# fp32 for y in the early tiles, splits only where they are needed, and another order of the third expert's units

## The chip, the cores and the metric

One core of one Trainium2 chip. The metric is the device time of one execution in microseconds; the profile is that of one execution of the same program. PE is the matrix engine, PEld its weight loads, DVE VectorE, ACT ScalarE, POOL GpSimd, SP the sync engine.

## The reference, cut to what matters

```python
# attention: B, H, S, D = 4, 8, 768, 48; a state of D x D per head, complex decay
scale = np.minimum(mag, 0.999) / (mag + 1e-06)
for t in range(S):
    S_re, S_im = ar * S_re - ai * S_im + k[t] (x) v[t], ar * S_im + ai * S_re
    y[t] = q[t] @ S_re
# first mixture, x (3072, 384), 8 experts of 1024, all of them on all rows
P = sinkhorn(exp(x @ w_gate - max), 8 rounds)          # columns and rows by turns
out = sum_e P[:, e] * (relu(x @ w1[e]) @ w2[e])
# second mixture: each row by the one expert of its largest logit
```

All is fp32. The kernel may split a value into two f16 parts, high and residue, and multiply three products of the parts.

## The kernel before, in words

The 3072 rows are 24 tiles of 128; tile n is step c = n // 4 of 128 time steps of batch b = n % 4. The kernel has a first and a second part. In the first, under `first_phase`, attention runs tile by tile and three of the eight experts of the first mixture (`RAW`) are computed without their factors, since the factors come only from the Sinkhorn loop at its end. The second part adds up these three with their factors, computes the other five, routes, and computes the second mixture.

In the first part the order of PE is that of the code (`manual_schedule`); DVE, ACT and the DMA queues are ordered by a planner, which follows priorities (`high_priority` shifts them) and the order of emission.

- `prep(u)` does a pair of tiles (u = 0 and 1 alone): decay, the scans over 128 steps, and WW, from which `stack` builds Q and K of a tile by DMA (SP's queue) in one of two buffers. It is a generator; its labels ("d", "s", "c1", ...) say how far it is. The planes, WW and v16 have one buffer each.
- `scales(u, ss)` turns the sums of squares of q, k and v into powers of two, and carries a bound of the state.
- `tile_attn(n)` has five steps: scores of heads 0 to 3 (ps, L393), masked and split into sc (L396 to L399); the same of heads 4 to 7; residues of S and Q (L402, L403), and K transposed (pk, kt); y (L420) out of three f16 products of Q and S (from tile 4 on) and three of sc and v; U (L427, fp32) and the new state.
- `emit_x` scales y's rows, splits them, transposes them into xg and computes the gate's logits.
- `tile_unit(e, n, wt, L)` is one expert on L tiles: for L = 2 four z steps (18 matmuls of 256 columns each) and two y steps (24 of 384), so six steps. `work` is the queue of units, `step(k)` emits the next k steps. `add_work(n)` puts two units (experts 0 and 1) in the queue for a pair of tiles, and, once the third expert's weights are there (`third_ready`, after 25 pieces of `early2`, one per attention step from tile 4 on), up to two of the third expert's from the list `third`.
- Tiles 0 to 3 follow the written list of letters: S stack, t attention step, x a step of emit_x, A add_work, w a unit step, p, a, b a step of a prep, e a piece of the weights. From tile 4 on a loop does it: after each attention step unit steps, in tile n's loop the rest of emit_x of tile n - 1, and prep of the pair after.
- At the end: one unit step, the last units, one unit of the last pair ahead of the others, two units to their end; then `sinkhorn`, nine times a piece of it, a piece of expert 3's weights and one unit step; then the units that are left.

Of the kernel before, what the change touches and what calls it, by code (L numbers as in the profile page):

```python
# [8 lines left out]
F32 = mybir.dt.float32  # L9
# [4 lines left out]
ALU = mybir.AluOpType  # L14
# [5 lines left out]
P = 128  # L20
# [2 lines left out]
PR = 128  # L23
HEAD_OF_SLOT = [0, 2, 4, 1, 3, 5, 6, 7]
RAW = 3
NS1 = 12
NS = 28
NSX = 31
# [4 lines left out]
class Kernel:  # L33
# [215 lines left out]
    def prep_part(self, u, L, a, qk, T, r, A, X, v, v16, WW):  # L249
# [2 lines left out]
        R = 3 * L  # L252
        tt = nc.vector.tensor_tensor
        stt = nc.vector.scalar_tensor_tensor
        ss = self.sm.tile([P, 3], F32, name=f"ss{u}", tag="ss")
        yield from self.decay(u, a, X, r)
        for i, src in enumerate((qk[:, 0], qk[:, 1], v)):
            dst = X[:, 0].rearrange("p (n w) -> p n w", w=384) if i == 2 else X[:, 0]
# [1 line left out]
        yield "d"  # L260

        def scaled():
            sc = self.scales(u, ss)
            self.act(u, v16[:, 0], v, AF.Copy, scale=sc[:, 1:2])
            stt(out=v16[:, 1], in0=v, scalar=sc[:, 1:2], in1=v16[:, 0], op0=ALU.mult, op1=ALU.subtract)
            self.vs.update((u + k, (v[:, k], v16[:, :, k], sc)) for k in range(L))

        if u > 1:
# [71 lines left out]
    def scales(self, u, ss):  # L340


        nc = self.nc
        ts = nc.vector.tensor_scalar
        ps = self.pp.tile([P, 3], F32, name=f"qkv{u}", tag="ps")
        nc.tensor.matmul(ps, self.ones, ss, start=True, stop=True)
        h, sc = (self.sm.tile([P, 5], F32, name=f"{t}{u}", tag=t) for t in ("sch", "scs"))
        bound = self.bound[u // 2 % 2]
        ts(out=h[:, 0:3], in0=ps, scalar1=2.0 ** -60, scalar2=None, op0=ALU.max)
        ts(out=h[:, 0:3].bitcast(I32), in0=h[:, 0:3].bitcast(I32), scalar1=1, scalar2=0x7F800000,  # L350
           op0=ALU.logical_shift_right, op1=ALU.bitwise_and)
        ts(out=h[:, 0:3], in0=h[:, 0:3], scalar1=2.0 ** 64, scalar2=None, op0=ALU.mult)
        nc.vector.scalar_tensor_tensor(out=bound, in0=h[:, 1:2], scalar=h[:, 2:3], in1=bound, op0=ALU.mult, op1=ALU.add)
        ts(out=h[:, 3:4].bitcast(I32), in0=bound.bitcast(I32), scalar1=0x7F800000, scalar2=None, op0=ALU.bitwise_and)
        nc.vector.tensor_copy(h[:, 1:2], h[:, 2:3])
        ts(out=h[:, 2:3], in0=h[:, 3:4], scalar1=2.0, scalar2=None, op0=ALU.mult)
        nc.vector.reciprocal(out=sc[:, 0:3], in_=h[:, 0:3])
        ts(out=sc[:, 0:3], in0=sc[:, 0:3], scalar1=2.0 ** 14, scalar2=None, op0=ALU.mult)
        ts(out=sc[:, 3:4], in0=sc[:, 2:3], scalar1=h[:, 1:2], scalar2=2.0 ** -14, op0=ALU.mult, op1=ALU.mult)
        ts(out=sc[:, 3:4], in0=sc[:, 3:4], scalar1=sc[:, 0:1], scalar2=None, op0=ALU.mult)  # L360
        ts(out=sc[:, 4:5], in0=h[:, 3:4], scalar1=h[:, 0:1], scalar2=2.0 ** -27, op0=ALU.mult, op1=ALU.mult)
        return sc

# [9 lines left out]
    def tile_attn(self, n):  # L373

        nc = self.nc
        c, b = divmod(n, 4)
        ap, ap2 = self.ap, self.ap2
        Q, K = self.QK[n % 2][:, 0], self.QK[n % 2][:, 1]
        tt = nc.vector.tensor_tensor
        stt = nc.vector.scalar_tensor_tensor  # L380
        v, v16, scl = self.vs.pop(n)
        last = c == NC - 1
        if c > 0:
            Q16 = self.q16[:, 0:2048].rearrange("p (a h t) -> p a h t", a=2, h=8)
            S16 = self.q16[:, 2048:2816].rearrange("p (a w) -> p a w", a=2)
            nc.scalar.activation(S16[:, 0], self.S[b], AF.Copy, scale=scl[:, 2:3])
            nc.scalar.activation(Q16[:, 0], Q[:, :, 0:128], AF.Copy, scale=scl[:, 0:1])
        sc = ap.tile([P, 2, 2, 4, P], F16, name=f"sc{n}", tag="sc")
        for g in range(2):
            ps = self.pp.tile([P, 4, P], F32, name=f"ps{n}_{g}", tag="ps")  # L390
            for j in range(4):
                h = g * 4 + j
                nc.tensor.matmul(ps[:, j, :], K[:, h, 0:128], Q[:, h, 0:128], start=True, stop=True)  # L393
            with self.tc.high_priority(offset=200):
                sc32 = self.UV.rearrange("p c w -> p (c w)")[:, 0:512].rearrange("p (h t) -> p h t", h=4)
                stt(out=sc32, in0=ps, scalar=scl[:, 3:4], in1=self.mask[:, None, :].to_broadcast([P, 4, P]), op0=ALU.mult,  # L396
                    op1=ALU.mult)
                nc.scalar.copy(sc[:, g, 0], sc32)
                tt(out=sc[:, g, 1], in0=sc32, in1=sc[:, g, 0], op=ALU.subtract)  # L399
            yield  # L400
        if c > 0:
            stt(out=S16[:, 1], in0=self.S[b], scalar=scl[:, 2:3], in1=S16[:, 0], op0=ALU.mult, op1=ALU.subtract)  # L402
            stt(out=Q16[:, 1], in0=Q[:, :, 0:128], scalar=scl[:, 0:1], in1=Q16[:, 0], op0=ALU.mult, op1=ALU.subtract)  # L403
        if not last:
            kt = ap.tile([P, 8, PR], F32, name=f"kt{n}", tag="kt")
            for g in range(2):
                pk = self.pp.tile([P, 4, PR], F32, name=f"pk{n}_{g}", tag="ps")
                for j in range(4):
                    nc.tensor.transpose(pk[:, j, :], K[:, g * 4 + j, 0:128], self.id32[:PR, :PR])
                nc.scalar.copy(kt[:, g * 4:g * 4 + 4, :], pk)  # L410
        yield
        y = self.pp.tile([P, 384], F32, name=f"y{n}", tag="ps")
        cols = [slice(HEAD_OF_SLOT[s] * 48, HEAD_OF_SLOT[s] * 48 + 48) for s in range(8)]
        own = [slice(s * 48, s * 48 + 48) for s in range(8)]
        for s in range(8):
            z = [(0, 0), (0, 1), (1, 0)]
            mm = [(Q16[:, i, s, :], S16[:, j, own[s]]) for i, j in z] if c > 0 else []
            mm += [(sc[:, s // 4, i, s % 4, :], v16[:, j, cols[s]]) for i, j in z]
            for i, (l, r) in enumerate(mm):
                nc.tensor.matmul(y[:, cols[s]], l, r, start=(i == 0), stop=(i == len(mm) - 1))  # L420
        self.pend = self.emit_x(n, y, scl[:, 4:5])
        next(self.pend)
        yield
        if not last:
            U = self.pp.tile([PR, 384], F32, name=f"U{n}", tag="ps")
            for s in range(8):
                nc.tensor.matmul(U[:, own[s]], kt[:, s, :], v[:, cols[s]], start=True, stop=True)  # L427
            UV = self.UV
            if c == 0:
                nc.scalar.copy(UV[:, 0], U)  # L430
            else:
                tt(out=UV[:, 0], in0=U, in1=self.S[b], op=ALU.add)
            nc.scalar.copy(UV[0:48, 1], UV[64:112, 0])
            nc.scalar.copy(UV[64:112, 1], UV[0:48, 0])
            e4 = UV.rearrange("p c (h e) -> p c h e", e=48)
            tt(out=e4, in0=e4, in1=self.QK[n % 2][:, :, :, 128:129].to_broadcast([PR, 2, 8, 48]), op=ALU.mult)
            tt(out=self.S[b], in0=UV[:, 0], in1=UV[:, 1], op=ALU.add)
        yield
# [660 lines left out]
    def first_phase(self):  # L1099
# [5 lines left out]
        with ExitStack() as ctx:  # L1105
# [3 lines left out]
            with ExitStack() as actx:  # L1109
# [24 lines left out]
                def add_work(n):  # L1134
# [7 lines left out]
                    if n % 2 == 1:  # L1142
                        third.append(n - 1)
                        if third_ready:
                            for _ in range(2):
                                if third:
                                    k = third.pop(0)
                                    work.append(self.tile_unit(2, k, self.wts[2], 2))

                self.WW = WW = {}  # L1150
                self.vs = {}
                first = [self.prep(u) for u in range(2)]
                prep = None
                for e in range(RAW):
# [7 lines left out]
                attn, pend, self.pend = {}, {}, None  # L1162
                at = None
                for what in """w a a a b a w e e a a e g w e w a e a e S0 e e b b b t0 b b r2 b w e t0 w t0 e w e e t0 x0
                      p t0 p A0 b S1 p x0 b t1 e w t1 e w t1 t1 w e w w e r4 S2 t1 e w e x1 t2 p A1 e w t2
                      w p x1 e t2 t2 w w p x2 t2 S3 e w p w x2 e t3 t3 e w A2 w t3 t3 A3 w w t3 x3 e w e x3""".split():
                    n = int(what[1:] or 0)
                    if what == "e":
                        next(early, None)
# [23 lines left out]
                run(early)  # L1193
                for n in range(4):
                    run(pend[n])
                while at in (None, "d1", "d2", "d"):
                    at = next(prep)
                for n in range(4, NT):
# [22 lines left out]
                    for i, _ in enumerate(self.tile_attn(n)):  # L1221
                        if early2 is not None and n > 3 and next(early2, True):
                            early2 = None
                            third_ready.append(True)
                        step(2 if i != 2 or len(work) > 4 else 1)
                        if ahead and i in (0, 2):
                            next(ahead, None)
                            if i == 0:
# [3 lines left out]
                    step(1)  # L1232
                was = len(work)
                add_work(NT - 1)
                work.insert(1, work.pop(was))
                run(work.pop(0))
                run(work.pop(0))
                late = self.getw(RAW, first_w)
                for _ in self.sinkhorn():
# [192 lines left out]
```

## Time and profile before

| | |
|---|---|
| time, median of 3 runs | 2129.28 us (2127.75 to 2132.78) |
| the profiled execution | 2127.34 us, span 2125.6 us |
| mean granted TensorE clock | 0.969 |
| busy: PE, PEld | 1935.3 us (91%), 1291.1 us (61%) |
| busy: DVE, ACT, POOL | 1285.5 us (60%), 887.7 us (42%), 202.4 us (10%) |
| busy tenths of PE in the first 8 of 40 slices | 1 4 6 8 9 6 8 9 |
| of DVE in the same | 8 8 9 9 9 9 9 8 |

The span runs from the first to the last instruction; the time of an execution has a little around it. A matmul's record is longer than the time until the next one starts, so lengths of PE work are read from start to start. The first part ends at about 889 us.

### The profile page before, as it was taken

To read this page: it belongs to the slowest core of one execution; us is meant where nothing else is said; L and a number is where in the kernel's file an instruction comes from. 1 tells how busy PE (TensorE), PEld (TensorE's weight loads), DVE (VectorE), ACT (ScalarE), POOL (GpSimd) and SP (SyncE) were. 2 spreads that over 40 slices of the span, in tenths; PEclk is the share of its full clock that TensorE was granted. 3 is DMA by queue.
4 is the path that set the end of the run, shared out by engine and by line. 5 is a ranking of instruction groups with operands and counts; after the bars stand their busy time and mean duration, and the time that the engine had idled before them with its cause. 6 is when DMAs were issued, how large, how long until landed. Compare 5 with 4: busy or idle time off the path is not lost.

```text
span 2125.6 us, 38747 instructions
## 1 busy us (share of the span) xinstructions
PE 1935.3 (91%) x15202; PEld 1291.1 (61%) x15202; DVE 1285.5 (60%) x3008; ACT 887.7 (42%) x1678; POOL 202.4 (10%) x311
## 2 busy tenths in 40 slices
PE   1468968999999996989999999999999999989998
PEld 1357757777778774635555555555555555567885
DVE  8899999988895326155434443443444355565886
ACT  5665655555454323243433433333334223355111
POOL 1000000000000000101100110110011010100005
PEclk9689889999999998989999999999999999999999
DMA  4323342422223102174311330231133200144222
GB/s 164 116 77 115 102 124 70 133 70 73 65 72 111 62 24 75 57 246 142 120 60 60 119 119 30 90 119 60 60 119 112 97 31 16 43 141 144 102 84 91
DMA packets 72927, 197.33 MB, mean 93 GB/s; under 512 B 10467, under 2 KB 54511, under 8 KB 67872
## 3 DMA queue, kind: packets, MB, share of 16 engines
q0 software_dynamic: 21808, 104.85, 14.2%
q1 hardware_dynamic: 50928, 89.88, 13.8%
q8 instruction: 127, 2.08, 0.4%
q14 instruction: 64, 0.52, 0.1%
HBM read 122.74 MB, written 53.71 MB: 83 GB/s over the span
## 4 chain that ended last, share of the span: by engine, by line
PE 53%; DMA 3%; DVE 2%; issue 1%; ACT 1%; SPq 1%; POOL 0%; DVEq 0%; POOLq 0%; ACTq 0%
PE ym L531 21%; PE z L520 20%; PE y L871 5%; PE z L856 4%; DMA rr<-rawd 1%; DMA late<-srt 1%; PE yt L566 1%; SPq L588 1%; PE zt L555 1%; DVE wt L134 0%; PE pt L651 0%; DMA st<-in_w_dram 0%; DVE acc L599 0%; ACT x L839 0%; DVE h L577 0%
## 5 line engine op out<-in xcount | busy, mean ns | idle before, releaser
L531 PE MATMUL ym<-wt,h 128*128 128x384 f16 x2880 | 477.5, 326 | 0.0
L531 PEld LDWEIGHTS <-h 128*128 128x128 f16 x2880 | 280.4, 98 | 184.8
L520 PEld LDWEIGHTS <-wt 128*128 128x128 f16 x2160 | 211.4, 99 | 262.9 <-issue 22.6
L577 DVE SCALAR_TENSOR_TENSOR h<-z,h 128x512 f16<-128x512 f32 (+1 forms) x352 | 212.2, 604 | 244.6 <-ACT h L576 237.2
L576 ACT ACTIVATE h<-z 128x512 f16<-128x512 f32 (+1 forms) x352 | 184.7, 526 | 373.3 <-PE z L520 242.2
L555 PE MATMUL zt<-xg,wt 128*128 128x256 f16 (+1 forms) x2736 | 303.2, 270 | 0.0
L566 PE MATMUL yt<-wt,ht 128*128 128x384 f16 x1728 | 290.4, 326 | 3.7 <-DVE ht L577 3.3
L555 PEld LDWEIGHTS <-wt 128*128 128x128 f16 x2736 | 259.4, 100 | 30.3
L520 PE MATMUL z<-xl,wt 128*128 128x512 f16 x1080 | 244.8, 386 | 14.1 <-DVE h L577 10.9
L520 PE MATMUL z<-xg,wt 128*128 128x512 f16 x1080 | 238.6, 379 | 0.0
L566 PEld LDWEIGHTS <-ht 128*128 128x128 f16 x1728 | 167.8, 98 | 111.9 <-DVE ht L577 5.9
L604 DVE SCALAR_TENSOR_TENSOR acc<-ym,pf,acc 128x384 f32<-128x384 f32 x120 | 74.0, 617 | 264.4 <-PE ym L531 264.4
L577 DVE SCALAR_TENSOR_TENSOR ht<-zt,ht 128x512 f16<-128x512 f32 x144 | 98.8, 686 | 73.6 <-ACT ht L576 72.9
L856 PE MATMUL z<-x,late 128*128 128x128 f16 x2016 | 130.6, 219 | 9.7 <-DVE late L845 7.0
L393 PE MATMUL ps<-QK 128*128 128x128 f32 x384 | 61.8, 310 | 84.4 <-DMA QK<-WW 79.9
L856 PEld LDWEIGHTS <-late 128*128 128x128 f16 x2016 | 120.0, 98 | 24.5 <-DVE late L845 8.9
L871 PE MATMUL y<-wq,h 128*128 x672 | 126.9, 326 | 2.7 <-issue 2.5
L576 ACT ACTIVATE ht<-zt 128x512 f16<-128x512 f32 x144 | 84.7, 592 | 86.4 <-PE zt L555 85.8
L124 ACT ACTIVATE wm<-st 128x1024 f32<-128x1024 f32 x48 | 50.7, 1057 | 142.7 <-DMA st<-in_w_dram 133.0
L393 PEld LDWEIGHTS ps<-QK 128*128 128x128 f32 x384 | 54.3, 217 | 85.6 <-DVE A L279 30.4
L583 POOL DMA_DIRECT2D rawd<-raw x72 | 39.0, 541 | 669.4 <-ACT raw L582 652.9
L582 ACT COPY raw<-yt 128x384 f32<-128x384 f32 x72 | 34.1, 473 | 115.5 <-PE yt L566 115.4
(318 smaller groups left out, 2241.7 us busy)
## 6 DMA issues: line engine op xcount, KB each, us to landing
st<-in_w_dram POOLq DMA_DIRECT2D x28, 1536.0 KB
QK<-WW SPq DMA_DIRECT2D x96, 145.1 KB, 3.4
rawd<-raw POOLq DMA_DIRECT2D x72, 192.0 KB
w1d<-wm POOLq DMA_DIRECT2D x64, 192.0 KB
w2d<-wm POOLq DMA_DIRECT2D x32, 384.0 KB
wq<-w2d SPq DMA_DIRECT2D x4, 3072.0 KB, 10.9
wq<-w1d SPq DMA_DIRECT2D x4, 3072.0 KB, 10.3
a<-in_att_dram SPq DMA_DIRECT2D x24, 384.0 KB, 3.8
```

What stands on the lines that cost most here:

```text
L124: nc.scalar.activation(junk, st[:, q * 1024:(q + 1) * 1024], AF.Square, accum_out=ss[:, q:q + 1])
L393: nc.tensor.matmul(ps[:, j, :], K[:, h, 0:128], Q[:, h, 0:128], start=True, stop=True)
L520: nc.tensor.matmul(z, w1[:, hw, k, f * P:(f + 1) * P], xg[:, hx, k, :], start=(i == 0), stop=(i == 8))
L531: nc.tensor.matmul(y, hs[f][:, hh, i * P:(i + 1) * P], w2[:, hw, f, :], start=(j == 0), stop=(j == 23))
L555: nc.tensor.matmul(z[:, f], w1[:, hw, k, o:o + P], xg[:, hx, k, :], start=(j == 0), stop=(j == 8))
L566: nc.tensor.matmul(y, hs[f // fz][:, hh, f % fz, i * P:(i + 1) * P], w2[:, hw, f, :], start=(j == 0), stop=(j == 23))
L576: nc.scalar.activation(h[:, 0], z, AF.Relu)
L577: nc.vector.scalar_tensor_tensor(out=h[:, 1], in0=z, scalar=0.0, in1=h[:, 0], op0=ALU.max, op1=ALU.subtract)
L583: nc.gpsimd.dma_start(out=self.rawd[e][n], in_=r)
L604: self.nc.vector.scalar_tensor_tensor(out=acc, in0=y, scalar=self.pf[:, e, n:n + 1], in1=acc, op0=ALU.mult, op1=ALU.add)
L856: nc.tensor.matmul(z[:, f], wc[:, hw, k, f * P:(f + 1) * P], x[:, hx * 3 + k, :], start=(i == 0), stop=(i == 8))
L871: nc.tensor.matmul(y, h[:, hh, f, :], w2[:, bass.ds(r * 1536 + (hw * 2 + f) * 384, 384)], start=(i == 0), stop=(i == 5))
```

## The change

Two bounds are new: `SPLITQ` = 8 and `SPLITV` = 12. Below tile 8 nothing is split in attention: scores are masked into fp32, y is Q times S and sc times v in fp32. From 8 to 11 Q and S are split, sc and v are not. From 12 all is as before. `scales` gets shorter accordingly, and below u = 4 it runs after tile 3 (`norms`), with four buffers for its sums. In the list of letters one p stands earlier, one is left out, and two e are added. The unit steps of an attention step fall to one (two at y) until the third expert is ready, and from tile 14 on, the last pair apart, one of its units is added a pair.

```diff
+SPLITQ, SPLITV = 8, 12
@@ prep_part
-        ss = self.sm.tile([P, 3], F32, name=f"ss{u}", tag="ss")
+        ss = self.sm.tile([P, 3], F32, name=f"ss{u}", tag="ss", bufs=4)
 ...
-            sc = self.scales(u, ss)
-            self.act(u, v16[:, 0], v, AF.Copy, scale=sc[:, 1:2])
-            stt(out=v16[:, 1], in0=v, scalar=sc[:, 1:2], in1=v16[:, 0], op0=ALU.mult, op1=ALU.subtract)
+            sc = None
+            if u < 4:
+                self.norms.append((u, ss))
+            else:
+                sc = self.scales(u, ss)
+            if u >= SPLITV:
+                self.act(u, v16[:, 0], v, AF.Copy, scale=sc[:, 1:2])
+                stt(out=v16[:, 1], in0=v, scalar=sc[:, 1:2], in1=v16[:, 0], op0=ALU.mult, op1=ALU.subtract)
@@ scales, after bound
+        if u < SPLITQ:
+            return None
 ...
-        ts(out=sc[:, 3:4], in0=sc[:, 2:3], scalar1=h[:, 1:2], scalar2=2.0 ** -14, op0=ALU.mult, op1=ALU.mult)
-        ts(out=sc[:, 3:4], in0=sc[:, 3:4], scalar1=sc[:, 0:1], scalar2=None, op0=ALU.mult)
+        if u < SPLITV:
+            ts(out=sc[:, 3:4], in0=sc[:, 2:3], scalar1=sc[:, 0:1], scalar2=None, op0=ALU.mult)
+        else:
 ...
@@ tile_attn
-        if c > 0:
+        qs = scl is not None
+        if qs:
 ...
-                stt(out=sc32, in0=ps, scalar=scl[:, 3:4], in1=self.mask[:, None, :].to_broadcast([P, 4, P]), op0=ALU.mult,
-                    op1=ALU.mult)
-                nc.scalar.copy(sc[:, g, 0], sc32)
-                tt(out=sc[:, g, 1], in0=sc32, in1=sc[:, g, 0], op=ALU.subtract)
+                if not qs:
+                    tt(out=sc8[:, g * 4:g * 4 + 4], in0=ps, in1=mask, op=ALU.mult)
+                else:
+                    stt(out=sc32 if split else sc8[:, g * 4:g * 4 + 4], in0=ps, scalar=scl[:, 3:4], in1=mask,
+                        op0=ALU.mult, op1=ALU.mult)
+                if split:
+                    nc.scalar.copy(sc[:, g, 0], sc32)
+                    tt(out=sc[:, g, 1], in0=sc32, in1=sc[:, g, 0], op=ALU.subtract)
 ...
-            mm = [(Q16[:, i, s, :], S16[:, j, own[s]]) for i, j in z] if c > 0 else []
-            mm += [(sc[:, s // 4, i, s % 4, :], v16[:, j, cols[s]]) for i, j in z]
+            mm = [(Q16[:, i, s, :], S16[:, j, own[s]]) for i, j in z] if qs else [(Q[:, s, 0:128], self.S[b][:, own[s]])] * (c > 0)
+            mm += [(sc[:, s // 4, i, s % 4, :], v16[:, j, cols[s]]) for i, j in z] if split else [(sc8[:, s, :], v[:, cols[s]])]
@@ first_phase
-                            for _ in range(2):
+                            for _ in range(2 if n < 14 or n == NT - 1 else 1):
 ...
+                for u, ss in self.norms:
+                    self.scales(u, ss)
 ...
-                        step(2 if i != 2 or len(work) > 4 else 1)
+                        step(2 if i == 3 or third_ready and (i != 2 or len(work) > 4) else 1)
 ...
-                work.insert(1, work.pop(was))
-                run(work.pop(0))
+                if was:
+                    work.insert(1, work.pop(was))
+                    run(work.pop(0))
                 run(work.pop(0))
```

## Rows read from the trace of the kernel before

**Rows 1.** The page's totals: busy us, share of the span, instructions.
```profile
PE 1935.3 (91%) x15202; PEld 1291.1 (61%) x15202; DVE 1285.5 (60%) x3008; ACT 887.7 (42%) x1678; POOL 202.4 (10%) x311
```

**Rows 2.** Stages: length, busy us of PE, PEld, DVE, ACT, POOL; clock, DMA, GB/s.
```profile
0.00:43.60 43.60, 2.18 (x8) 1.95 (x9) 36.85 (x152) 26.19 (x60) 7.66 (x20) 1.00 0.47 161
43.60:122.00 78.40, 28.12 (x251) 25.23 (x251) 67.90 (x180) 46.09 (x91) 2.14 (x4) 0.69 0.41 120
122.00:215.00 93.00, 84.63 (x894) 70.26 (x894) 87.75 (x211) 57.24 (x107) 4.88 (x9) 0.96 0.34 95
215.00:284.50 69.50, 46.86 (x452) 38.59 (x453) 65.96 (x158) 43.23 (x81) 3.78 (x7) 0.82 0.40 117
284.50:341.00 56.50, 50.18 (x471) 41.57 (x472) 55.26 (x133) 34.89 (x64) 2.71 (x5) 0.92 0.39 115
341.00:420.00 79.00, 78.27 (x751) 62.05 (x750) 76.97 (x166) 47.13 (x89) 3.79 (x7) 0.98 0.28 85
420.00:773.00 353.00, 349.39 (x3269) 277.28 (x3268) 241.59 (x556) 161.42 (x299) 21.07 (x39) 1.00 0.25 74
```

**Rows 3.** PE in order of time, its waits: start, us, line, [idle before, releaser].
```profile
122.06 2.04 PE L393 MATMUL ps<-QK 128*128 128x128 f32 x8 [30.26 <-DMA QK<-WW]
...
219.96 2.05 PE L393 MATMUL ps<-QK 128*128 128x128 f32 x8 [4.55 <-DVE xs L451]
...
284.53 2.04 PE L393 MATMUL ps<-QK 128*128 128x128 f32 x8 [18.12 <-DMA QK<-WW]
...
338.13 0.50 PE L468 MATMUL pt<-id,xt 128*128 128x128 f16 x3 [5.53 <-ACT xt L463]
```

**Rows 4.** PE in order of time: y of tiles 2, 6; U; a unit's y step.
```profile
133.51 0.76 PE L420 MATMUL y<-v,sc 128*128 128x48 f16 x24 [0.49 <-DVE lg L477]
134.11 4.06 PE L566 MATMUL yt<-wt,ht 128*128 128x384 f16 x24
...
211.78 3.63 PE L427 MATMUL U<-v,kt 128*128 128x48 f32 x16
...
231.14 0.23 PE L420 MATMUL y<-q 128*128 128x48 f16 x3
...
232.34 2.13 PE L555 MATMUL zt<-xg,wt 128*128 128x256 f16 x18
...
238.32 1.88 PE L427 MATMUL U<-v,kt 128*128 128x48 f32 x16
240.04 4.06 PE L566 MATMUL yt<-wt,ht 128*128 128x384 f16 x24
243.94 2.13 PE L555 MATMUL zt<-xg,wt 128*128 128x256 f16 x18
```

**Rows 5.** DVE by line and shape, 0 to 341 us: busy us, mean ns | idle before.
```profile
L396 DVE SCALAR_TENSOR_TENSOR UV<-ps,scs,mask 128x512 f32<-128x512 f32 x21 | 15.7, 745 | 3.5 <-PE ps L393 3.5
L399 DVE TENSOR_TENSOR sc<-UV,sc 128x512 f16<-128x512 f32 x21 | 14.4, 686 | 0.4 <-ACT sc L398 0.4
L403 DVE SCALAR_TENSOR_TENSOR q<-QK,scs,q 128x1024 f16<-128x1024 f32 x7 | 8.9, 1278 | 1.1 <-ACT q L387 1.1
L265 DVE SCALAR_TENSOR_TENSOR v<-v,scs,v 128x768 f16<-128x768 f32 x5 | 5.1, 1011 | 0.1
L402 DVE SCALAR_TENSOR_TENSOR q<-S,scs,q 128x384 f16<-128x384 f32 x7 | 4.3, 609 | 0.0
L359 DVE TENSOR_SCALAR scs<-scs,sch 128x1 f32<-128x1 f32 x7 | 1.5, 209 | 0.0
L355 DVE COPY sch<-sch 128x1 f32<-128x1 f32 x7 | 1.0, 142 | 0.0
```

**Rows 6.** PE in order of time in the Sinkhorn loop: its two long waits.
```profile
816.38 0.59 PE L904 MATMUL pc<-cs,ones 128*128 128x8 f32 x2 [5.56 <-DVE cs L902]
824.25 0.58 PE L177 MATMUL wsum<-wss,ones 128*128 128x3 f32 x2 [7.27 <-ACT wt L124]
```

More of the change, by code (lines that the diff above doesn't have):

```diff
@@ L358, in scales @@
         ts(out=sc[:, 0:3], in0=sc[:, 0:3], scalar1=2.0 ** 14, scalar2=None, op0=ALU.mult)
-        ts(out=sc[:, 3:4], in0=sc[:, 2:3], scalar1=h[:, 1:2], scalar2=2.0 ** -14, op0=ALU.mult, op1=ALU.mult)
-        ts(out=sc[:, 3:4], in0=sc[:, 3:4], scalar1=sc[:, 0:1], scalar2=None, op0=ALU.mult)
+        if u < SPLITV:
+            ts(out=sc[:, 3:4], in0=sc[:, 2:3], scalar1=sc[:, 0:1], scalar2=None, op0=ALU.mult)
+        else:
+            ts(out=sc[:, 3:4], in0=sc[:, 2:3], scalar1=h[:, 1:2], scalar2=2.0 ** -14, op0=ALU.mult, op1=ALU.mult)
+            ts(out=sc[:, 3:4], in0=sc[:, 3:4], scalar1=sc[:, 0:1], scalar2=None, op0=ALU.mult)
         ts(out=sc[:, 4:5], in0=h[:, 3:4], scalar1=h[:, 0:1], scalar2=2.0 ** -27, op0=ALU.mult, op1=ALU.mult)
@@ L388, in tile_attn @@
         sc = ap.tile([P, 2, 2, 4, P], F16, name=f"sc{n}", tag="sc")
+        split = n >= SPLITV
+        sc8 = sc.rearrange("p g a h t -> p (g a h t)").bitcast(F32).rearrange("p (h t) -> p h t", h=8)
         for g in range(2):
@@ L395, in tile_attn @@
                 sc32 = self.UV.rearrange("p c w -> p (c w)")[:, 0:512].rearrange("p (h t) -> p h t", h=4)
-                stt(out=sc32, in0=ps, scalar=scl[:, 3:4], in1=self.mask[:, None, :].to_broadcast([P, 4, P]), op0=ALU.mult,
-                    op1=ALU.mult)
-                nc.scalar.copy(sc[:, g, 0], sc32)
-                tt(out=sc[:, g, 1], in0=sc32, in1=sc[:, g, 0], op=ALU.subtract)
+                mask = self.mask[:, None, :].to_broadcast([P, 4, P])
+                if not qs:
[6 more added lines that the diff above has]
+                    tt(out=sc[:, g, 1], in0=sc32, in1=sc[:, g, 0], op=ALU.subtract)
             yield
-        if c > 0:
+        if qs:
             stt(out=S16[:, 1], in0=self.S[b], scalar=scl[:, 2:3], in1=S16[:, 0], op0=ALU.mult, op1=ALU.subtract)
@@ L416, in tile_attn @@
             z = [(0, 0), (0, 1), (1, 0)]
-            mm = [(Q16[:, i, s, :], S16[:, j, own[s]]) for i, j in z] if c > 0 else []
-            mm += [(sc[:, s // 4, i, s % 4, :], v16[:, j, cols[s]]) for i, j in z]
+            mm = [(Q16[:, i, s, :], S16[:, j, own[s]]) for i, j in z] if qs else [(Q[:, s, 0:128], self.S[b][:, own[s]])] * (c > 0)
+            mm += [(sc[:, s // 4, i, s % 4, :], v16[:, j, cols[s]]) for i, j in z] if split else [(sc8[:, s, :], v[:, cols[s]])]
             for i, (l, r) in enumerate(mm):
                 nc.tensor.matmul(y[:, cols[s]], l, r, start=(i == 0), stop=(i == len(mm) - 1))
-        self.pend = self.emit_x(n, y, scl[:, 4:5])
+        self.pend = self.emit_x(n, y, scl[:, 4:5] if qs else 1.0)
         next(self.pend)
@@ L1150, in first_phase @@
                 self.WW = WW = {}
-                self.vs = {}
+                self.vs, self.norms = {}, []
                 first = [self.prep(u) for u in range(2)]
@@ L1164, in first_phase @@
                 for what in """w a a a b a w e e a a e g w e w a e a e S0 e e b b b t0 b b r2 b w e t0 w t0 e w e e t0 x0
-                      p t0 p A0 b S1 p x0 b t1 e w t1 e w t1 t1 w e w w e r4 S2 t1 e w e x1 t2 p A1 e w t2
-                      w p x1 e t2 t2 w w p x2 t2 S3 e w p w x2 e t3 t3 e w A2 w t3 t3 A3 w w t3 x3 e w e x3""".split():
+                      p t0 p A0 b S1 p x0 p b t1 e w t1 e w t1 t1 w e w w e r4 S2 t1 e w e e e x1 t2 p A1 e w t2
+                      w p x1 e t2 t2 w w p x2 t2 S3 e w w x2 e t3 t3 e w A2 w t3 t3 A3 w w t3 x3 e w e x3""".split():
                     n = int(what[1:] or 0)
```

## The prediction

> **What bounds the kernel now.** I read the totals first, then a table by stage, then the waits of the matrix engine (PE), then the costs of the lines that the change touches.
>
> The totals say PE 91%, VectorE (DVE) 60% [rows 1]; the stages say something else [rows 2]. I cut the first part at the points where PE resumed after a wait. From 341 us to 773 us PE is busy 427.7 of 432 us: there only PE's own work counts. Before 341 us it is busy 212.0 us and idle 129.0, while DVE is busy 313.7 us (92%; 95% from 122 us on). What PE waits for there is DVE's product: the DMA that stacks Q and K after the decay scans (30.3 us at tile 2, 18.1 at tile 8), or a row scale of an earlier tile (4.6, 5.5) [rows 3]. So the first 341 us go at DVE's pace with one exception: from 122 to 215 us PE is at 91% and DVE at 94%, both near full. PE's order is fixed by the code, so its idle time can't be filled with later units.
>
> By the code, the point at 341 us is tile 10's second attention step, and the units that PE has done by then are the same in both versions. I counted the queue with the step rules of each: it is empty at the end of tile 9 both times, and 17 steps are left after tile 10. So the first part ends earlier by what the way to that point loses, plus or minus what PE's own work grows after it.
>
> **The change part by part.**
>
> *y in fp32 (added on PE).* Before, a tile's y takes 24 f16 matmuls in batch-first tiles 0 to 3 (133.51 to 134.11 us, 0.60 us) and 48 later (231.14 to 232.34, 1.20 us), 25 ns each. The trace has no y in fp32, but U is the same shape, a 128x128 fp32 stationary tile against 48 fp32 columns: 8 such matmuls, two records each, go from 238.32 to 240.04, 1.72 us or 215 ns each [rows 4]. So one fp32 matmul (215 ns) replaces three f16 ones (75 ns). Tiles 0 to 3: 1.72 - 0.60 = +1.12 us each; 4 to 7 (two fp32 per head): 3.44 - 1.20 = +2.24; 8 to 11: 0.60 + 1.72 - 1.20 = +1.12. Sum 18.0 us, 15.7 of it in tiles 0 to 9. Bounds: the sum is nothing where PE would have waited, 18.0 if all of it stands in PE's way, and twice that after idle stretches (U took 3.63 us at 211.78, just after a stretch of stalls).
>
> The page FP8 and Floating Point Precision of the Trainium skill (section TensorE Precision Notes) says that true fp32 is four passes through the array. Four times the 25 ns of an f16 record would be 100 ns, the extra 3 us in all, and the forecast about 2105 us. The row of U shows two records and 215 ns per matmul, so the row's price stands.
>
> *Splits that go (DVE).* Each tile below 12 loses the subtract behind the scores, 2 x 0.686 us, and the multiply with the mask stays, writing fp32 (I keep its 0.745 us; the plain subtract of the same size, 0.686, is the lower bound [rows 5]). Tiles 4 to 7 lose the residues of Q and S, 1.28 + 0.61. The residue of v goes in every prep up to 10, 1.01 us a pair, about 0.6 in the two single ones (the price of S's residue, which has their width). The scale chain loses 8 short operations of 0.14 to 0.21 us (1.4 us a prep) for u = 0, 1, 2, 4, 6, and for u below 4 the rest of it, one matmul and four DVE operations, moves behind tile 3, where it comes back and waits for nothing. By stage, as durations: to 43.6 us 2.7 (u = 0, all of its chain); 43.6 to 122: 2.7 scores + 3.0 (u = 1, 2 chains with what is put off, about 4.2) + 1.6 of v, 7.9 in all; 122 to 215 (tiles 2 to 5): 5.5 + 3.8 + 1.0 + 2.8 - 2.1 that comes back = 11.0; 215 to 284.5 (tiles 6, 7): 2.7 + 3.8 + 2.0 + 0.2 = 8.7; 284.5 to 341 (tiles 8, 9): 2.7 + 1.0 + 0.2 = 4. Together 34 us. Small operations overlap their neighbours, so 28 is the lower end.
>
> y now reads v and Q themselves: v's buffer is held until U and that of Q and K until the multiply at the tile's end in both versions, so no later load waits for it.
>
> *ScalarE* loses the copies in f16 that go with each of these. It is at about 60% in these stages [rows 2] and I give it nothing of its own; the shorter way from scores to y only takes away short waits.
>
> *Steps per attention step.* Until the third expert's weights are ready (in tile 8) PE now does 6 unit steps a tile instead of 9. The sum of steps to tile 9 is unchanged, so this costs no work: it takes units from tiles 4 and 5, where PE is full, to later tiles, where it stood waiting for the stack. One y step of 3.9 us (240.04 to 243.94 [rows 4]) crosses from before 284.5 us to after it. The moved p and e entries of the preamble shift when preps are issued, not how much; I give them nothing, with +-2 us as bounds from the 4.6 us that PE waited on such a chain.
>
> *Third expert's last units.* From tile 14 on one unit a pair enters the queue instead of two. The queue never runs dry after tile 10 in my count (14 steps at the least), so PE has the same work, in another order. At the end 7 steps instead of 10 run ahead of the Sinkhorn loop, in the loop the same nine, after it 21 instead of 15. The stalls in the loop (5.6 and 7.3 us) come from DVE's column sums and from the next weights' norm [rows 6], not from an empty queue, so they stay. Value 0; bounds -13 us (both stalls gone) and +8 us (three steps, two of about 2 us and one of 3.9, no longer in front of the loop, if the norm of the next weights then comes late).
>
> *What the stages become.* To 43.6 us: DVE paces, -2. To 122: 7.9 off a DVE busy 67.9 of 78.4, PE has room; -5. 122 to 215: DVE falls to 76.8, but PE needs 84.6 + 6.7 (tiles 2 to 5) = 91.3 of 93.0; with almost no stall left -1. 215 to 284.5: DVE 66.0 - 8.7 = 57.3, PE 46.9 + 4.5 - 3.9 = 47.5; DVE paces with about 2 us of its 3.5 us idle left: 59.5, -10. 284.5 to 341: DVE 51.3, PE 50.2 + 2.2 + 3.9 = 56.3 at a granted clock of 0.92, some of which comes back with the stall: 55.5, -1. Sum -19. After 341 us tiles 10 and 11 add 2.2 to a full PE: -17. The profiled execution took 2127.3 us (span 2125.6 and 1.7 around it), the median of the runs is 2129.3. So 2110.3 on the profiled one and 2112 against the median; I say 2111.
>
> So a DVE relief of 34 us turns into half, because the fp32 passes meet the stage where PE is already full.
>
> **The rivals.**
>
> *Full conversion.* DVE runs ahead in the stage where PE is full, and spends it in the next; then nearly all of 34 us comes through, less 2.2: 2097. For it: DVE gets 16 us of slack from 122 to 215. Against: the prep's planes and WW have a single buffer, so the next prep can't start far ahead; PE's own need to 341 us.
>
> *PE takes DVE's place (slower).* From 122 us on every fp32 pass stands in the chain from scores over y to the row scale and U, and the waits for the stacked Q and K stay as they are, because the preps set them and not the scores. Then 13.4 us (tiles 2 to 9) and 2.2 are paid in full, against the 7 won before 122 us: 8.6 more, 2138. It decides once less than 9 us of the 37 us that PE idles from 122 to 341 us goes. For it: PE is at 91% in the first of these stages. Against: DVE at 95% with 24 us less to do. Were PE the pace everywhere in the first part, nothing would be won and all 18.0 us paid: 2147; the stages speak against that up to 341 us and for it from there on [rows 2].
>
> The page Perfetto Trace Analysis of the Trainium skill (section Identifying the Most-Contended Engine) says to relieve the engine with the highest occupancy first. By the totals [rows 1] that is PE, to which this change adds work: the 2147 of the sentence before, by that reading.
>
> *It cancels.* The waits from 122 to 341 us only shrink by what the fp32 passes fill. Then the 7 us before 122 us stand against 2.2 in tiles 10 and 11 and the 3.9 of the moved step: -1, 2128. For it: PE near full from 122 to 215 us and at 89% from 284.5 to 341. Against: the stage between, at 67%, where DVE alone paces.
>
> **How the numbers follow.** My forecast 0.56 (own range 2104 to 2119), full conversion 0.22, cancels 0.13, slower 0.07 by the chain and 0.02 by all 18 us. A difference below about 0.2% (4 us) can't be told from none here. Faster by more: forecast, full conversion and a little of the third, 0.80; within: 0.11; slower: 0.09. The range from 2095 to 2128 leaves out the slower cases and what lies beyond full conversion.
>
> **What would show it.** In the profile after: DVE without the 0.686 us subtracts before tile 12; y in fp32 at about 1.7 us per 8 matmuls; PE back without waits at about 321 us instead of 341, with idle time before it near 95 us instead of 129; PE's busy time to that point up by some 15 us; the wait before tile 8 well below 18 us; from there to the Sinkhorn loop the same length within 3 us; the loop's two stalls still there. The prediction is wrong if the stack waits of tiles 4 to 9 are as long as before (the slower rival), if 122 to 215 us shrinks by 8 us or more (full conversion), or if the end of the first part moves by something that the first 341 us don't show.

## The result, and the profile after

The changed kernel takes 2112.34 us (median, 2109.17 to 2114.29) against 2130.69 for the one before on the same chip: ratio 0.9913 [0.9895, 0.9932]. The forecast was 2111. The profiled execution took 2112.55 us with a span of 2110.9, 14.7 below the 2125.6 of before.

The totals of the page (busy us, share of the span, instructions), beside [rows 1]:

```profile
PE 1946.9 (92%) x15074; PEld 1304.5 (62%) x15074; DVE 1254.8 (59%) x2927; ACT 865.3 (41%) x1639; POOL 202.9 (10%) x311
```

To compare like with like I cut both traces at the same points of PE's program: first scores of tile 2, of tile 6, of tile 8, and the unit after tile 10's second scores. Columns as in [rows 2]. Before:

```profile
0.00:122.06 122.06, 30.31 (x260) 27.21 (x260) 104.81 (x331) 72.28 (x151) 9.80 (x24) 0.80 0.43 134
122.06:219.96 97.90, 85.03 (x894) 70.51 (x895) 92.20 (x223) 59.46 (x111) 4.88 (x9) 0.94 0.37 104
219.96:284.53 64.57, 46.45 (x451) 38.34 (x451) 61.48 (x148) 41.04 (x78) 3.78 (x7) 0.84 0.37 105
284.53:340.89 56.36, 50.06 (x470) 41.43 (x471) 55.12 (x133) 34.75 (x64) 2.71 (x5) 0.92 0.39 115
```

After:

```profile
0.00:120.77 120.77, 30.62 (x240) 27.89 (x240) 98.70 (x290) 72.54 (x150) 9.82 (x24) 0.82 0.43 136
120.77:213.47 92.70, 90.64 (x850) 76.69 (x851) 84.26 (x217) 47.24 (x92) 4.90 (x9) 0.96 0.40 112
213.47:271.23 57.76, 45.28 (x396) 38.70 (x396) 47.94 (x118) 33.98 (x67) 3.27 (x6) 0.94 0.40 110
271.23:327.20 55.97, 54.86 (x478) 44.56 (x479) 54.23 (x137) 29.37 (x55) 3.25 (x6) 0.97 0.38 111
```

The stages shrink by 1.3, 5.2, 6.8 and 0.4 us: 13.7 in all, which is nearly the whole gain (14.7). The third column of busy time is the one to read. DVE has 313.6 us of work to that point before and 285.1 after, 28.5 less; its idle time went from 27.3 to 42.1, 14.8 more. So half of DVE's relief came out as time and half as waiting of DVE itself.

PE in order of time, its waits before tile 2, tile 8 and the unit, beside [rows 3], and the two in the Sinkhorn loop, beside [rows 6]:

```profile
107.02 0.59 PE L178 MATMUL wsum<-wss,ones 128*128 128x3 f32 x2 [17.54 <-ACT wt L125]
120.77 2.05 PE L407 MATMUL ps<-QK 128*128 128x128 f32 x8 [12.50 <-DMA QK<-WW]
271.23 2.05 PE L407 MATMUL ps<-QK 128*128 128x128 f32 x8 [12.48 <-DMA QK<-WW]
324.85 0.49 PE L487 MATMUL pt<-id,xt 128*128 128x128 f16 x6 [0.38 <-DVE xt L483]
327.20 4.09 PE L574 MATMUL zt<-xg,wt 128*128 128x256 f16 x36 [0.73 <-ACT xg L490]
786.62 0.60 PE L923 MATMUL pc<-cs,ones 128*128 128x8 f32 x2 [5.52 <-DVE cs L921]
794.09 0.59 PE L178 MATMUL wsum<-wss,ones 128*128 128x3 f32 x2 [6.88 <-ACT wt L125]
```

The waits of 4.55 (tile 6) and 5.53 us (tile 10) are gone, that of tile 8 fell from 18.12 to 12.48, and the 30.26 us before tile 2 are still 30.0, in two pieces.

What DVE waited for up to that point, in us, times and longest; before:

```profile
DVE UV L396 <- PE ps L393: 3.5, 2, 3.1
DVE wt L168 <- ACT wt L167: 1.4, 1, 1.4
DVE ht L577 <- ACT ht L576: 1.0, 3, 0.4
```

After (xm's line had no such wait before):

```profile
DVE xm L466 <- ACT xt L464: 5.8, 5, 1.7
DVE sc L412 <- PE ps L407: 5.7, 3, 4.3
DVE ht L596 <- ACT ht L595: 4.7, 5, 2.0
DVE wt L169 <- ACT wt L168: 4.1, 1, 4.1
```

These four lines grew by some 14 us together, about the 14.8 of new idle time: three of them wait for ScalarE, which does the half before DVE's in row scales, relu and weight splits. ScalarE in its turn waited for PE, for y at the start of a row scale and for z at a relu; before:

```profile
ACT xt L445 <- PE y L420: 0.7, 1, 0.7
ACT ht L576 <- PE zt L555: 9.6, 10, 1.5
```

After:

```profile
ACT xt L464 <- PE y L439: 9.5, 7, 2.5
ACT ht L595 <- PE zt L574: 27.8, 15, 5.8
```

### The profile page after: what moved, and what is told of

The parts are those of the page before. It is cut to its first block, busy times and chain, and to the rows that moved or that the text cites. A ratio compares the mean times of both kernels' runs of the same rounds, so it can differ in the third digit from the quotient of the medians.

```text
span 2110.9 us, 38353 instructions
## 1 busy us (share of the span) xinstructions
PE 1946.9 (92%) x15074; PEld 1304.5 (62%) x15074; DVE 1254.8 (59%) x2927; ACT 865.3 (41%) x1639; POOL 202.9 (10%) x311
## 4 chain that ended last, share of the span: by engine, by line
PE 42%; issue 11%; DMA 3%; DVE 3%; POOL 1%; ACT 1%; SPq 0%; POOLq 0%; DVEq 0%; ACTq 0%
PE ym L550 20%; PE z L539 20%; POOL out_dram L899 1%; DMA rr<-rawd 1%; PE yt L585 1%; DVE acc L618 1%; DMA acc<-rawd 1%; PE zt L574 1%; DVE wt L135 1%; DMA late<-srt 0%; DMA out_dram<-ya,tok 0%; PE pt L670 0%; DVE h L596 0%; ACT h L595 0%; DMA st<-in_w_dram 0%
## 5 line engine op out<-in xcount | busy, mean ns | idle before, releaser
L539 PE MATMUL z<-xl,wt 128*128 128x512 f16 x1080 | 241.9, 383 | 15.6 <-DVE h L596 12.4
L407 PE MATMUL ps<-QK 128*128 128x128 f32 x384 | 57.3, 297 | 51.9 <-DMA QK<-WW 51.9
```

What stands on the lines that cost most here:

```text
L539: nc.tensor.matmul(z, w1[:, hw, k, f * P:(f + 1) * P], xg[:, hx, k, :], start=(i == 0), stop=(i == 8))
```

## The experiments

Marks in the table are us in each profile: PE's first scores of tile 2, the unit after tile 10's scores, the way from the one to the other, the second part's first matmul. Ratios are to the kernel before on the same chip.

```
kernel                       ratio [95%]              tile 2   unit     way     2nd part
before                       1                        122.06   340.89   218.8   892.44
after                        0.9913 [0.9895, 0.9932]  120.77   327.20   206.4   879.61
after again (e12)            0.9921 [0.9904, 0.9939]  120.25   324.78   204.5   879.50
e1 arithmetic alone          0.9936 [0.9921, 0.9952]  118.61   327.76   209.2   880.14
e2 schedule alone            1.0027 [1.0015, 1.0038]  121.42   346.12   224.7    903.80
e3 third expert as before    0.9916 [0.9901, 0.9930]  120.35   325.17   204.8   879.02
e4 y step ahead              0.9890 [0.9873, 0.9906]  118.06   319.97   201.9   873.25
e5 y twice                   1.0005 [0.9993, 1.0018]  121.16   347.38   226.2   899.22
e6 DVE back                  0.9954 [0.9936, 0.9972]  119.40   333.81   214.4   886.18
e7 steps as before           0.9945 [0.9928, 0.9962]  118.78   328.14   209.4   880.76
e8 y step, split from 10     0.9902 [0.9885, 0.9920]  119.06   322.58   203.5   874.44
e9 f16 fill                  0.9933 [0.9917, 0.9949]  121.26   327.99   206.7   879.67
e10 y of high halves         0.9891 [0.9874, 0.9907]  119.38   322.62   203.2   874.38
e11 list as before           0.9947 [0.9930, 0.9963]  116.65   337.37   220.7   889.64
```

Nine of these run the same program up to tile 2 (after, again, e3 to e9; in e6 alone DVE has two added subtractions ahead of it) and reach it between 118.06 and 121.26 us, so a mark of one profile is good to about 1.6 us; the way from tile 2 on is the steadier measure (204.5 to 206.4 in after, again and e3, mean 205.3).

**Which part does it.** e1 is after with the old list, step rule and third-expert order; e2 is before with the new ones; e3 undoes the third expert's alone:

```diff
-                            for _ in range(2 if n < 14 or n == NT - 1 else 1):
+                            for _ in range(2):
```

> The new arithmetic (fp32 up to tile 7, Q and S split to 11) with the old list of letters, the old unit steps and the old order of the third expert. Theory (DVE relief pays, but only where PE is not full): tiles 4 and 5 again carry 9 unit steps and the dearer y, so PE paces there and the wait for the stack at tile 8 stays long; a part of the 18 us is lost: 2118 to 2123, wait at tile 8 over 15 us. Rival 1 (the schedule makes the gain): 2128 to 2138, since the fp32 passes cost and nothing is won. Rival 2 (the relief alone makes it): 2110 to 2114.

> The old arithmetic with the new list, unit steps and order of the third expert. Theory: DVE still paces up to about 340 us, so PE's second step of tile 10 stays within 4 us of 341 us and the time within 0.25% of before: 2125 to 2133. Rival 1 (the schedule makes the gain): 2112 to 2118.

> The changed kernel, but the third expert's units enter the queue two a pair as before. Theory: the queue never runs dry after tile 10 either way, so the same work in another order: within 3 us of the changed kernel, 2109 to 2116, both stalls of the Sinkhorn loop still 5 to 8 us. Rival (the longer tail makes part of the gain, seen as the 2 us that the second part wins in its first 60 us): 2115 to 2120.

The arithmetic alone brings the first part as far as the whole change does, without the wait before tile 8 that I expected; its median is 3 us above that of e3 on the same chip (2119.29 against 2116.23). The schedule alone makes the old arithmetic slower: the unit comes at 346.1 us and the time is 0.27% up, both just outside what I expected. That refutes the reading that the schedule makes the gain. The third expert's order is worth nothing that can be measured.

**List and steps.** e11 puts back the old list, e7 the old step rule:

```diff
-                        step(2 if i == 3 or third_ready and (i != 2 or len(work) > 4) else 1)
+                        step(2 if i != 2 or len(work) > 4 else 1)
```

> after with the old rule of steps per attention step (9 unit steps a tile instead of 6 before the third expert's weights are there); list and third expert as after. The prediction gave the new rule 3.9 us: a y step of that length crosses behind the stack's wait of tile 8. If that holds, tile 10 comes 3 to 5 us later than in after and the ratio to after is about 1.002. Rival: the relieved DVE lets the stack come in time whichever way the steps are dealt (the kernel with the arithmetic alone has no such wait): tile 10 within 2 us of after's, ratio 1.000 within 0.001.

> after with the old list of letters for the first 122 us; steps and third expert as after. The prediction gave the list nothing (within 2 us). The kernel with the arithmetic alone reached tile 2 at 118.6 us with one wait of 30.2, after at 120.8 with 12.5 and 17.5. If the list is worth nothing: tile 10 within 2 us of after's 327.2, ratio 0.9915 within 0.0015. Rival (the moved entries cost what tile 2 shows): 2 to 3 us earlier.

e7 takes 4.1 us more from tile 2 to the unit than the mean of 205.3. That is not the 3.9 of the prediction, although e7's expectation takes it so: there the new rule puts a y step behind tile 8's wait, which lengthens the last stage in its sum and stands as a cost in its rival "It cancels", so by it the old rule would have gained time. In e7 the wait before tile 8 is gone; from tile 6 to tile 8 (columns as above):

```profile
214.81:270.23 55.42, 53.62 (x419) 44.65 (x420) 47.18 (x119) 32.88 (x63) 3.78 (x7) 0.90 0.41 121
```

On the way PE idles 7.8 us against 15.7 in after, but is busy 10.8 us longer (201.6 against 190.8). That is the clock. The time lost to it (busy time times one minus the granted clock, summed over slices of 2 us from 120 us to the unit) is 15.1 us in e7 and 11.4 in e1, but 4.8, 4.8 and 4.5 in after, again and e3; the last section shows where it fell.

e11 missed both expectations: the old list wins 3 us at tile 2 and then loses 15. In it six weight splits come after tile 2 instead of ahead of it, and the third expert's splits cost DVE more waiting (7.3 us against 4.1 in after):

```profile
DVE wt L169 <- ACT wt L168: 7.3, 2, 6.1
```

Old list with old steps (e1), new with old (e7) and old with new (e11) stand at 0.9936, 0.9945 and 0.9947; both new (after, again, e3) at 0.9913, 0.9921 and 0.9916. So list and steps belong together and are worth about a quarter of a per cent only as a pair, on top of the arithmetic; single intervals touch, the two groups of three don't overlap in their medians. With the old steps (e1, e7) more is lost to the clock than is won in waits. With the old list and the new steps it takes 10.5 us, and the wait before tile 8 is 14.43 us; why the list matters there was not settled.

**Whose microsecond counts.** e6 puts DVE work back, whose result nobody reads, in tiles 4 to 7; e5 doubles y's fp32 matmuls there; e9 adds f16 matmuls that y overwrites:

```diff
# e6
+        if 4 <= n < 8:
+            tt(out=self.q16[:, 2432:2816], in0=self.S[b], in1=self.S[b], op=ALU.subtract)
+            tt(out=self.q16[:, 1024:2048]..., in0=Q[:, :, 0:128], in1=Q[:, :, 0:128], op=ALU.subtract)
# e5
-            for i, (l, r) in enumerate(mm):
+            for _ in range(2 if 4 <= n < 8 else 1):
+                for i, (l, r) in enumerate(mm):
 ...
# e9
+        for _ in range(58 if 4 <= n < 8 else 0):
+            nc.tensor.matmul(y[:, 0:P], self.id16, self.id16, start=True, stop=True)
```

> y's fp32 matmuls of tiles 4 to 7 are issued twice, one more time what this change added or more (after: 3.56 us a tile, so +3.4 us each and 13.8 us in all on PE); DVE's work is untouched. Theory A (the relief of DVE passes only where PE has room): after has 2 us of PE idle from 121 to 209 us, so tiles 4 and 5 are paid nearly in full, and 12 us from 209 to 271 us, so tiles 6 and 7 go into it: first part +5 to +9 us, ratio to after 1.002 to 1.004, the wait before tile 8 well below 12 us. Rival B (DVE sets the first part throughout, PE's passes are free): tile 10 within 2 us of after's. Rival C (y stands in DVE's chain and is paid everywhere): +12 us or more.

> In tiles 4 to 7 two subtractions whose result nobody reads are put back on DVE at the sizes of the residues that went (Q 1.28 us, S 0.61 us): +7.6 us on DVE, nothing on PE. Theory A (PE full to 209 us, DVE the pace from 209 to 271): those of tiles 4 and 5 cost little, those of 6 and 7 delay the stack before tile 8 by their 3.8 us: tile 10 later by 2 to 5 us, ratio to after 1.001 to 1.0025. Rival B (DVE sets the pace all the way, a microsecond of DVE is one of the end): +7 us. Rival C (PE is the pace by now, DVE is hidden): 0.

> Ahead of y in tiles 4 to 7, 58 f16 matmuls of 128x128 by 128 columns (identity by identity, overwritten by y) go on PE: at about 60 ns each (36 with 128 columns take 2.17 us in after) +3.5 us a tile, the same 13.8 us that the doubled y was meant to add, but f16. The doubled fp32 y cost 20 us at tile 10: after the first 16 or so of its 32 fp32 matmuls the records went from 0.39 to 0.63 us a pair and PE's granted clock was 0.50 to 0.57 for some 10 us, four times. Theory (the long run of fp32 passes lowers the clock): here the clock stays at 1.00 after y, and tile 10 comes 1 to 9 us later than in after (13.8 less what goes into the 12.5 us of wait before tile 8). Rival (any added PE time is paid like that, because the chain is PE's): +14 us or more, as with the doubled y.

In e6 the subtractions take 7.1 us of DVE (those of Q 4.9), 1.1 of it ahead of tile 2. The way is 9.1 us longer (214.4 against 205.3), the second part starts 6.6 to 7.2 us later than in after, again and e3, and the wait before tile 8 grew by 6.2: rival B, DVE sets the pace all the way, about one microsecond for one.

```profile
278.60 1.62 PE L407 MATMUL ps<-QK 128*128 128x128 f32 x6 [18.66 <-DMA QK<-WW]
```

In e9 the added matmuls take 3.24 us a tile, 13.0 in all; the first of them, and the y behind:

```profile
179.97 3.40 PE L433 MATMUL y<-id 128*128 128x128 f16 x58
183.21 0.37 PE L441 MATMUL y<-S,QK 128*128 128x48 f32 x2
```

They cost 1.5 us on the way; the wait before tile 8 is gone, so PE had that room. The median is 3.7 us above that of again on the same chip (2117.02 against 2113.37; the intervals overlap). In e5 the 13.8 us that were meant cost 21. That lies in rival C ("+12 us or more"), but not for its reason, since e9 holds up y by nearly as much. PE in order of time in e5, at tile 4's y:

```profile
183.86 0.39 PE L440 MATMUL y<-S,QK 128*128 128x48 f32 x2
184.08 0.40 PE L440 MATMUL y<-v,sc 128*128 128x48 f32 x2
184.31 0.61 PE L440 MATMUL y<-S,QK 128*128 128x48 f32 x2
184.72 0.63 PE L440 MATMUL y<-v,sc 128*128 128x48 f32 x2
...
189.41 6.61 PE L586 MATMUL yt<-wt,ht 128*128 128x384 f16 x24
195.85 2.13 PE L575 MATMUL zt<-xg,wt 128*128 128x256 f16 x18
```

In the middle of the run the pairs go from 0.39 to 0.63 us, and 24 f16 matmuls behind it take 6.61 us instead of 4.06. Stages there (e5, columns as above):

```profile
180.00:184.00 4.00, 4.00 (x39) 4.00 (x37) 4.00 (x6) 2.93 (x5) 0.00 (x0) 1.00 0.02 4
184.00:194.00 10.00, 10.00 (x44) 7.63 (x44) 4.62 (x10) 4.56 (x10) 0.00 (x0) 0.52 0.00 0
```

and in e9:

```profile
184.00:194.00 10.00, 10.00 (x82) 8.25 (x82) 9.60 (x16) 5.88 (x12) 0.54 (x1) 1.00 0.05 20
```

PE is busy throughout, and in e5 its granted clock is 0.52, the lower level (1.2 GHz), where e9 has 1.00. It happens at each of the four doubled y. The time lost to the clock (the sum described at e7) is 20.9 us in e5 and 4.8 in after. PE's busy time on the way is 29.6 us longer than in after (220.4 against 190.8), 16.1 of it by the clock; its idle time is 9.8 shorter, and 19.8 us are left (226.2 against 206.4). e5 and e9 differ in the kind of the added matmuls, and in their place: between y's own in e5, ahead of them in e9. So it was the long run of fp32 matmuls of 48 columns in which the clock fell; type and width were not tried apart.

**What the fp32 passes cost.** e10 reads the upper halves in place, so y up to tile 7 is cheap on PE and DVE's work is that of after:

```diff
+        hi = lambda a: a.bitcast(mybir.dt.bfloat16).rearrange("p (w z) -> p w z", z=2)[:, :, 1]
...
+            if not split and not qs:
+                mm = [(hi(l), hi(r)) for l, r in mm]
```

> In tiles 0 to 7 y takes only the upper 16 bits of v, S, Q and of the scores, read as bf16 in place: DVE and ScalarE do what they do in after, and y's 64 fp32 matmuls and 32 more become bf16 ones (the lower halves are left out of y). PE loses up to 18 us (1.72 to about 0.2 us per 8). Theory A (the fp32 passes are what halves DVE's relief): tile 10 comes 6 to 12 us earlier than in after's 327.2, ratio to before 0.986 to 0.989. Rival B (from 121 us on the stack of Q and K, so DVE, sets tile 10): the waits before tiles 6 and 8 grow by what PE saves, tile 10 within 3 us of after's.

The way is 2.0 us shorter than the mean of 205.3, the unit 2 to 5 us earlier, the start of the second part some 5, and the median 5.4 us below that of again on the same chip (2107.95 against 2113.37). From tile 2 to tile 6 (columns as above), then PE's wait before tile 8, which grew:

```profile
119.38:205.13 85.75, 83.78 (x802) 69.51 (x803) 80.36 (x205) 46.26 (x91) 4.34 (x8) 0.93 0.38 105
263.77 2.05 PE L407 MATMUL ps<-QK 128*128 128x128 f32 x8 [14.61 <-DMA QK<-WW]
```

PE's busy time to the unit fell by 12.4 us (221.4 to 209.0), although the clock took 9.8 instead of 4.8, and between a sixth and four tenths of that came through: at tile 10 nearer to rival B, in the ratio (0.9891) at the edge of theory A. ScalarE's wait for y is nearly gone, and DVE's wait at xm no longer appears:

```profile
ACT xt L467 <- PE y L442: 0.9, 2, 0.7
```

**Two versions.** e4 runs one unit step more ahead of tile 8; e8 also splits tiles 10 and 11 in full, as before the change (SPLITV = 10):

```diff
+                        step(2 if i == 3 or n == 7 and i == 4 or third_ready and (i != 2 or len(work) > 4) else 1)
```

> The changed kernel, but after the last attention step of tile 7 two unit steps are emitted instead of one, so that expert 1's last y step of tiles 4 and 5 (3.9 us) stands before the wait for tile 8's stack and not behind it. Theory (that wait, 12.5 us, is set by the stack's DMAs, and from there PE is full): the wait shrinks by 3.9 us to about 8.6 and the end comes 3.9 us earlier: 2108 to 2109, ratio to before about 0.990. Rival (what DVE has to do for tile 8 waits on that y step or on the units behind it, so the stall moves on): no change, 2112.

> The kernel with the y step moved ahead, and tiles 10 and 11 split in full as before (24 f16 matmuls at 25 ns for v's part instead of 8 fp32 ones at 215 ns: -1.1 us of PE a tile where PE is full). If the tiles past 10 go at PE's pace: 2.2 us below the kernel with the y step alone, about 2108, ratio to after about 0.998. Rival: DVE is busy 54 of 56 us just before tile 10, and gets v's residue (1.0 us) and four splits of the scores (0.69 us each) back there or soon after: no gain or 1 to 2 us lost.

e4 cuts the wait before tile 8 to 8.04 us and the way by 3.4. In e8 the stretch from the unit to the second part is 551.9 us against 553.3 in e4: of the 2.2 us that I expected 1.4 show, within the spread of the marks, and the total shows none. e4 is the lowest of all, about 0.2 to 0.3% under after; the intervals overlap.

> The changed kernel once more, as the measure for the other three on the same chip: 0.9913 of before within its interval.

It came out at 0.9921, within the first interval.

## Why the prediction was right, and where not

**Right: what bounds it.** "The first 341 us go at DVE's pace": a microsecond of DVE is about one of the way (e6), one of PE is a tenth to four tenths (e9, e10). The two rivals in which PE takes over are refuted by the gain itself and by e9. Of the other two, full conversion would have shortened 122 to 215 us by 8 or more (0.7 at the same cut, below), and cancelling would have left the time as it was. The rule that I quoted from Perfetto Trace Analysis of the Trainium skill (section Identifying the Most-Contended Engine) makes an exception that I left out: for PE it goes by the busy share of the weight loads, not by that of the matmuls. By the totals that is 61% beside DVE's 60% [rows 1], so the rule names PE by a hair only. The trace decides for the stages, 2112.

**Right: the price of fp32.** In after 16 records, 8 matmuls, begin at 152.88 us and the next line at 154.60, 1.72 us as U's row gave:

```profile
152.88 1.88 PE L439 MATMUL y<-v,sc 128*128 128x48 f32 x16
154.60 0.65 PE L585 MATMUL yt<-wt,ht 128*128 128x384 f16 x3
```

PE's busy time to the unit rose by 9.4 us, not the 15 named: 4.4 come back from the clock (the sum described at e7 is 9.2 us before and 4.8 after), and about 1 stays open.

**Right in size, in part in its reason: the half.** "A DVE relief of 34 us turns into half, because the fp32 passes meet the stage where PE is already full." The relief was 28.5, near the lower end given (28); half of it came out as time. Where PE was full the reason holds: from tile 2 to where PE stopped ahead of tile 6 the stretch went from 93.4 to 92.7 us. Without the passes (e10) the stretch to tile 6 is 5 to 7 us shorter than in after and again; but the way from there to the unit is 3.8 longer, so that only 2 to 5 us more come through in all. The rest is idle time of DVE, most of it directly behind ScalarE, to which I gave "nothing of its own". That doesn't show ScalarE to be the limit: its work fell (207.5 to 183.1 us up to the unit), it waited more for PE's y and z, and DVE's wait at xm is gone where y is cheap (e10). Which engine of this chain sets the time was not separated; no run changed ScalarE's work.

**Wrong: the way to tile 2.** Up to it I had -7 and got -1.3: of 10.6 us off DVE 4.5 went to six weight splits (0.745 us each) that the new list takes from behind tile 2 to ahead of it, which leaves the 6.1 of the table, and 4.8 of these became idle time of DVE. The list was priced at 0 within 2. The stages from tile 2 to tile 8 gave -12.0 against -11 together; cut where PE stopped ahead of tile 6 (215.41 us before), -0.7 against -1 and -11.4 against -10. So the unit came 13.7 us earlier (16.1 and 15.7 in again and e3), not 19.

**Right on average, with luck in the sum: behind the unit.** For tiles 10 and 11 I added 2.2. From the unit to the second part it is 551.6 us before and 552.4, 554.7 and 553.9 in after, again and e3, on average 2.1 more. The second part alone (by the code the same work) is 1233.2 us before and 1231.3 after, but varies from 1231 to 1239 between profiles. So the traced sum came out (-17 forecast, -14.7 in span) by an early miss of 5 us and a later one of 3 the other way, 1.9 of it within that spread. The medians differ by 18.4 us, as forecast; that closeness is partly luck.

**Right: the third expert's order** (0; e3) and the Sinkhorn stalls (5.52 and 6.88 us, still there).

**Wrong in its sign: the step.** The 3.9 us of the y step that crosses the wait stood as work added behind it; with the old rule the way is 4.1 us longer, not shorter (e7). The likeness of the two numbers is luck. The step's own price is right: moved ahead of the wait again, it gains 3.4 (e4). What the sum lacked is that the old rule leaves y and U without an f16 unit between them, and that the clock falls there.

## What to carry to other kernels

Read the pace from stages, then ask of a relieved engine whom it will wait for next, and whom that one waits for in turn: here DVE stood behind ScalarE, and ScalarE behind PE. To learn whose microsecond counts, add work rather than only remove it: 7 us on DVE cost 7 to 9, 13 us of f16 on PE 1.5 to 4, and about as much time in fp32 matmuls 21, so the kind of the added work matters too. Compare profiles over a stretch that starts behind the noise, not by absolute marks.

## What the runs showed of the hardware that was not expected

In runs of small fp32 matmuls PE's clock fell although the profile shows no idle time of PE there. In e5 that was a doubled y. In e7 the plain one was enough, where the old step rule leaves no f16 unit between tile 5's y and U. PE in order of time in e7 (busy 3.97 of 4.00 us from 207 to 211 us; the granted clock is 0.50 from 211 to 223):

```profile
209.90 0.42 PE L439 MATMUL y<-S,QK 128*128 128x48 f32 x2
210.12 0.62 PE L439 MATMUL y<-v,sc 128*128 128x48 f32 x2
...
211.40 3.61 PE L446 MATMUL U<-v,kt 128*128 128x48 f32 x16
214.81 2.04 PE L407 MATMUL ps<-QK 128*128 128x128 f32 x8
```

In after a unit's y step stands between the two, and the same U takes 1.88 us, the same scores 1.12:

```profile
207.85 4.06 PE L585 MATMUL yt<-wt,ht 128*128 128x384 f16 x24
211.75 1.88 PE L446 MATMUL U<-v,kt 128*128 128x48 f32 x16
213.47 1.12 PE L407 MATMUL ps<-QK 128*128 128x128 f32 x8
```

The page TensorE: Matmul & The Clock Gate of the Trainium skill (Part 1: The HAM clock gate) puts the fall of the clock down to PE having been idle. The waits before tile 8 agree with that (granted clock 0.50 from 264 to 270 us in after); e5 doesn't, since its profile shows PE busy 10.00 of 10.00 us in the slow stretch, and there the measurement decides. A profile's busy time only says that instructions were under way; how full they kept the engine no run here shows.
